# Scores in row halves with a 0/1 mask product, and a fixed order of engines and PSUM banks, in an attention and mixer kernel

## The chip, the cores and the metric

The kernel runs on one core of a Trainium2 chip. The metric is the device time of the slowest (here the only) core in microseconds, as the median of several executions. The span that a profile shows is some 2 us shorter than that execution's time, because it runs from the first to the last instruction of the program.

## The reference, cut to what matters

Two stages follow one another. The first is attention over 4 batches of 8 heads with 768 positions and head dimension 64, under a mask made of 32-position blocks. The second is a mixer on each batch: a product of rank 32 along the sequence, then a two-layer perceptron of widths 512, 2048 and 512.

```python
scores = scale * np.matmul(q, k.transpose(0, 1, 3, 2))      # 768 x 768 for each of 32 heads
scores = np.where(mask, scores, -1000000000.0)              # mask: 24 x 24 blocks of 32 x 32
attn = np.exp(scores - scores.max(-1, keepdims=True)); attn /= attn.sum(-1, keepdims=True)
x = np.matmul(attn, v)                                      # then heads side by side: 768 x 512
u = x + (x^T U V)^T                                         # rank 32
out = u + relu(u @ w_ch1) @ w_ch2
```

The kernel handles two heads at a time, a "pair": 16 pairs, four to a batch. While the pairs of batch b go through attention, the perceptron of batch b-1 runs in between.

## The kernel before

The mask lies in the contraction. A head's queries and keys have 64 rows. Below or above them stand 24 rows: a one-hot code of the block on one side and -240 for each block that is masked on the other. One matmul over all 128 rows then gives score plus mask, and one exponential of ScalarE finishes it (scale 0.125).

```python
drows = [slice(0, D), slice(D, P)]            # rows of head 0 and of head 1: D = 64, P = 128
mrows = [slice(D, D + NB), slice(0, NB)]      # the 24 mask rows of each
def scores(i, h, g):                          # 128 keys of one head, all 768 queries
    psc = pscp.tile([P, 2, 512], FP32, tag="psc", name="psc")       # two PSUM banks, two buffers
    for c in range(2):
        nc.tensor.matmul(psc[:, c, 0:HS],                           # HS = 384
            kT[:, h, g * P : (g + 1) * P], qT[:, h, c * HS : (c + 1) * HS], start=True, stop=True)
    nc.scalar.activation(out=est[:, g]..., in_=psc[:, :, 0:HS], func=AF.Exp, scale=0.125)
```

The other large parts are the value products (128x65), the two layers of the perceptron (`w1` with 384 columns, `w2` with 512), the relus, dealt by turns to ScalarE and VectorE, and the small steps of the mixer. Program order on TensorE is fixed by slots: one score step, then whatever is due. PSUM comes from three pools, and the order on the other engines is the scheduler's.

```python
def w1(jj, c):                                # ... four matmuls into one bank, then
    if c == 0: nc.scalar.activation(out=dst, in_=pt, func=AF.Relu)
    else:      nc.vector.tensor_scalar_max(out=dst, in0=pt, scalar1=0.0)
for h in range(2):                            # ... in the loop over pairs
    for g in range(T):
        pair.ests[h] = scores(i, h, g)
        at(slot - g + AVSLOT[g], lambda ...: pair.av(h, g))         # value products some slots later
        run_due()                             # ... and perceptron steps of the batch before
```

The softmax here doesn't subtract the row's maximum and nothing guards it: scores larger than these inputs give would overflow.

Of the kernel before, what the change touches and what calls it, by code (L numbers as in the profile page):

```python
# [16 lines left out]
P = 128  # L17
# [3 lines left out]
def kernel(  # L21
# [29 lines left out]
    NST = 2  # L51
# [14 lines left out]
    oh_np = np.zeros((P, T, D), dtype=np.float16)  # L66
    oh_np[cols % P, cols // P, blk] = 1.0

# [11 lines left out]
    oh_dr = nc.inline_tensor(oh_np, name="onehot_const")  # L80
# [6 lines left out]
    epool = ctx.enter_context(tc.tile_pool(name="epool", bufs=2))  # L87
    xpool = ctx.enter_context(tc.tile_pool(name="xpool", bufs=2))
    upool = ctx.enter_context(tc.tile_pool(name="upool", bufs=2))
    tpool = ctx.enter_context(tc.tile_pool(name="tpool", bufs=18))  # L90
# [3 lines left out]
    pscp = ctx.enter_context(  # L94
        tc.tile_pool(name="pscp", bufs=2, space=bass.MemoryType.PSUM)
    )
    psvp = ctx.enter_context(
        tc.tile_pool(name="psvp", bufs=1, space=bass.MemoryType.PSUM)
    )
    psmp = ctx.enter_context(  # L100
        tc.tile_pool(name="psmp", bufs=3, space=bass.MemoryType.PSUM)
    )

    def psm(shape, dtype):
        return psmp.tile(shape, dtype, tag="pm", name="pm")

    id16 = consts.tile([P, P], FP16)
    oh = consts.tile([P, T, D], FP16)
# [6 lines left out]
    qst = [consts.tile([P, 2, T, P], FP16, name=f"qst{i}") for i in range(NST)]  # L115


# [4 lines left out]
    kst = [consts.tile([P, 2, T, P], FP16, name=f"kst{i}") for i in range(NST)]  # L122
# [6 lines left out]

    def load_qk(i):  # L130
        b, hp = divmod(i, HP)
        last = None
        for src, st, nm in ((q, qst, "qld"), (k, kst, "kld")):
            ld = ldpool.tile([P, 2, T, D], FP32, tag="ld" + nm, name=nm)
            nc.sync.dma_start(
                out=ld,
                in_=src[b, 2 * hp : 2 * hp + 2].rearrange("h (p t) d -> p h t d", t=T),
            )
            if i < NPE:
                sts[i, nm] = stpool.tile([P, T, 2, D], FP16, tag="st" + nm, name="st" + nm)  # L140
                dst = sts[i, nm].rearrange("p t h d -> p h t d")
            else:
                dst = st[i % NST][:, :, :, 0:D]
            last = nc.gpsimd.tensor_copy(out=dst, in_=ld)  # L144
        return last

    def load_v(i):
        b, hp = divmod(i, HP)
        ld = ldpool.tile([P, 2, T, D], FP32, tag="ldv", name="vld")
        nc.sync.dma_start(  # L150
            out=ld,
            in_=v[b, 2 * hp : 2 * hp + 2].rearrange("h (p t) d -> p h t d", t=T),
        )
        nc.gpsimd.tensor_copy(out=vts[b % 2][:, 2 * hp : 2 * hp + 2, :, 0:D], in_=ld)  # L154
# [27 lines left out]
    for tile_ in (Ut, Vt):  # L182
        nc.gpsimd.memset(tile_, 0.0)
# [7 lines left out]
    def first_turn(h, n, c):  # L191
# [3 lines left out]
        elif c == 0:  # L195
            pt = pw[:, 1, 0:HS]
        else:
            pt = pscp.tile([P, 2, 512], FP32, tag="psc", name="psc")[:, 0, 0:HS]
# [9 lines left out]
    with tc.manual_schedule(  # L208
# [5 lines left out]
        pw = pscp.tile([P, 2, 512], FP32, tag="psc", name="psc")  # L214
# [7 lines left out]
        pks = [psvp.tile([P, HS], FP32, tag="pv", name="pv"), psm([P, HS], FP32)]  # L222
# [77 lines left out]

    def mask_columns():
        def both(ap):
            return ap[:, None].broadcast_to([P, 2, T, D])

        nc.sync.dma_start(out=oh, in_=oh_dr.ap())
        pb = psm([P, T, D], FP32)
        for t in range(T):
            nc.tensor.matmul(
                pb[:, t, :], ohT[:, t * P : (t + 1) * P], bias[0:NB, 0],
                start=True, stop=True,  # L310
            )
        nc.vector.tensor_copy(out=kst[0][:, 0, :, D:], in_=pb)
        nc.gpsimd.tensor_copy(out=kst[0][:, 1, :, D:], in_=kst[0][:, 0, :, D:])
        for i in range(NST):
            nc.gpsimd.tensor_copy(out=qst[i][:, :, :, D:], in_=both(oh))
            if i > 0:
                nc.gpsimd.tensor_copy(out=kst[i][:, :, :, D:], in_=kst[0][:, :, :, D:])
# [29 lines left out]

    def front(i):
        augs[i] = (qres[i % 2], kres[i % 2])
        for st, aug in zip((qst, kst), augs[i]):  # L350
            last = nc.sync.dma_start_transpose(
                aug.rearrange("d h (t p) -> d (h t) p", t=T),
                st[i % NST].rearrange("p h t d -> p (h t d)"),
# [23 lines left out]
    ests = {}  # L377

    def scores(i, h, g):
        qT, kT = augs[i]  # L380
        if g == 0:
            ests[h] = epool.tile([P, T, S], FP16, tag="est", name="est")
        est = ests[h]
        psc = pscp.tile([P, 2, 512], FP32, tag="psc", name="psc")
        for c in range(2):
            nc.tensor.matmul(  # L386
                psc[:, c, 0:HS],
# [5 lines left out]
            out=est[:, g].rearrange("k (c n) -> k c n", c=2), in_=psc[:, :, 0:HS],  # L393
            func=AF.Exp, scale=0.125,
        )
        return est

    class Batch:
        def __init__(self):
            self.xf = xpool.tile([P, T, HD], FP32, tag="xf", name="xf", bufs=3)  # L400
# [5 lines left out]
            self.tT = []  # L406


    class Pair:
        def __init__(self, i, bt):  # L410
            self.b, self.hp = divmod(i, HP)
            self.bt = bt
            self.ests = {}
            self.pu = {}
            self.xh = xpool.tile([P, T, P], FP16, tag="xh", name="xh", bufs=3)
            self.ch = slice(self.hp * P, (self.hp + 1) * P)
            self.xbar = NPE <= i < NPAIR - 1

        def av(self, h, g):

            head = 2 * self.hp + h
            if g == 0:
                self.pav = psvp.tile([P, T, D + 1], FP32, tag="pv", name="pv")
            pav, est = self.pav, self.ests[h]
            for sc in range(T):
                nc.tensor.matmul(  # L426
                    pav[:, sc, :],
                    est[:, g, sc * P : (sc + 1) * P],
                    vts[self.b % 2][:, head, g, 0 : D + 1],
                    start=(g == 0 and sc == 0), stop=(g == T - 1),  # L430
                    skip_group_check=True,
                )
            if g == T - 1:
                rcp = misc.tile([P, T], FP32, tag="rcp", name="rcp")
                nc.vector.reciprocal(out=rcp, in_=pav[:, :, D])  # L435
                for dst in (
                    self.xh[:, :, h * D : (h + 1) * D],
                    self.bt.xf[:, :, head * D : (head + 1) * D],
                ):
                    self.last = nc.vector.tensor_tensor(  # L440
                        out=dst, in0=pav[:, :, 0:D],
                        in1=rcp[:, :, None].broadcast_to([P, T, D]), op=ALU.mult,
                    )

        def mix(self):
            pa = psm([P, P], FP32)
# [5 lines left out]
            nc.vector.tensor_copy(out=self.bt.a16[:, self.ch], in_=pa)  # L452


        def ut_x(self, c):
            pu = self.pu[c] = psm([P, HS], FP32)
            for j in range(3):
                nc.tensor.matmul(
                    pu[:, j * P : (j + 1) * P], self.xh[:, 3 * c + j, :], id16,
# [3 lines left out]
        def ut_a(self, c):  # L463
# [6 lines left out]
            nc.vector.tensor_copy(  # L470
                out=self.bt.uT[self.hp][:, c * HS : (c + 1) * HS], in_=self.pu[c]
            )


        def add(self, c):
            if c == 0:
                self.u16 = xpool.tile([P, T, P], FP16, tag="u16", name="u16")
            pu = psm([P, 3, P], FP32)
# [7 lines left out]
            nc.vector.tensor_add(out=self.u16[:, ts, :], in0=self.xh[:, ts, :], in1=pu)  # L486
            nc.vector.tensor_add(out=xf, in0=xf, in1=pu)  # L487
            if c == 1 and self.xbar:
                nc.sync.dma_start_transpose(
                    self.bt.uT[self.hp].rearrange("c (t p) -> c t p", t=T),  # L490
                    self.u16.rearrange("p t c -> p (t c)"),
                )

        def turn(self):
            pt = psm([P, S], FP16)
# [4 lines left out]
            nc.vector.tensor_copy(out=self.bt.uT[self.hp], in_=pt)  # L500


    def mlp_steps(b, bt):
        def w1(jj, c):
            if c == 0:
                bt.tT.append(tpool.tile([P, S], FP16, tag="tT", name="tT"))
            pt = psm([P, HS], FP32)
            for cc in range(NCC):
                nc.tensor.matmul(  # L509
                    pt,  # L510
                    w1t[:, cc, jj * P : (jj + 1) * P],
                    bt.uT[cc][:, c * HS : (c + 1) * HS],
                    start=(cc == 0), stop=(cc == NCC - 1),
                )
            dst = bt.tT[jj][:, c * HS : (c + 1) * HS]
            if c == 0:
# [4 lines left out]
        hold = {}  # L521

        def w2(sc, part):
            if part == 0:
                hold[sc] = psm([P, HD], FP32)
                if b == 0:
                    nc.tensor.matmul(  # L527
                        hold[sc], Vt[:, sc, :], bt.a16, start=True, stop=False
                    )
            for jj in range(4 * part, 4 * part + 4):  # L530
                nc.tensor.matmul(  # L531
                    hold[sc],
                    bt.tT[jj][:, sc * P : (sc + 1) * P],
                    w2t[:, jj, :],
                    start=(b > 0 and jj == 0), stop=(jj == NJJ - 1),
# [193 lines left out]
```

## Time and profile before

| | before |
|---|---|
| time, median | 298.92 us (298.86 to 299.38) |
| PE busy, as the page models it | 98% |
| sum of all matmul spacings if none waited | 283 us |
| lost between the first and the last matmul start | 9.3 us, of which 7.7 us before 50 us |
| VectorE (DVE), ScalarE (ACT) busy | 142.0 us, 179.8 us |

The first fence is from the page of the kernel before: the span, the busy times of the engines, and the shares of the chain that ended last.

```profile
span 296.7 us, 6622 instructions
PE 291.4 (98%) x2775; PEld 182.3 (61%) x2775; DVE 142.0 (48%) x299; ACT 179.8 (61%) x261; POOL 50.2 (17%) x70
PE 87%; ACT 12%; issue 0%; DVE 0%
```

TensorE's work ends the kernel in 87% of the chain. But a busy PE is modelled, since matmuls overlap. The next lines are the costliest groups of the page (line, engine, operation, tiles, shapes, count; then busy us, mean ns of one, and idle time before them).

```profile
L392 ACT ACTIVATE est<-psc 128x768 f16<-128x768 f32 x192 | 149.6, 812 | 51.6 <-PE psc L386 50.7
L509 PE MATMUL pm<-uT,w1t 128*128 128x384 f16 x512 | 94.6, 326 | 0.0
L386 PE MATMUL psc<-qres,kres 128*128 128x384 f16 x384 | 93.5, 325 | 1.0 <-ACT est L392 0.7
L531 PE MATMUL pm<-w2t,tT 128*128 128x512 f16 x368 | 90.7, 379 | 0.0
L426 PE MATMUL pv<-vt,est 128*128 128x65 f16 x1152 | 55.7, 193 | 0.0
```

The mean of one matmul (325 ns for 384 columns) is its time from start to end, not what it costs in a stream. The cost is the distance to the next start. In the trace that is 162 ns for 384 columns, 215 ns for 512, 55 ns for 128 and 29 ns for 65. All "sums" below use these distances, and a "wait" is what a start comes later than that. The 384 score matmuls are thus 62 us.

The table by stretches shows where the kernel is bound by what. Its columns are the busy time of each engine, the clock, the DMA share and the rate.

```profile
core 0: us, PE busy (x) PEld busy (x) DVE busy (x) ACT busy (x) POOL busy (x), PEclk, DMA share, GB/s
0.00:16.00 16.00, 14.49 (x143) 8.52 (x144) 11.78 (x25) 12.34 (x18) 8.98 (x17) 1.00 0.75 239
16.00:44.00 28.00, 27.70 (x403) 20.99 (x401) 19.78 (x45) 27.98 (x40) 14.09 (x20) 1.00 0.90 255
50.00:297.00 247.00, 243.18 (x2165) 148.65 (x2162) 106.04 (x220) 134.41 (x197) 23.69 (x29) 1.00 0.46 114
```

From 16 to 44 us ScalarE is busy 27.98 of 28 us: the first batch has no perceptron to hide behind, so its exponentials set the pace. After 50 us only PE is full.

Two stretches of PE's timeline will be needed later (start us, length us, group, count, and in brackets a wait with its releaser). Six products with 24-row operands (they put mask values in columns) cost a gap before and after, although nothing holds them.

```profile
32.04 0.48 PE L386 MATMUL psc<-qres,kres 128*128 128x384 f16 x2
32.46 0.34 PE L308 MATMUL pm<-bias,small 24*128 24x64 f16 x6
32.74 0.35 PE L426 MATMUL pv<-vt,est 128*128 128x65 f16 x6
...
6.61 0.48 PE L386 MATMUL psc<-qres,kres 128*128 128x384 f16 x2
6.93 0.50 PE L281 MATMUL pm<-id,stqld 128*128 128x128 f16 x6
7.26 0.49 PE L386 MATMUL psc<-qres,kres 128*128 128x384 f16 x2
```

Two 384-column matmuls from 32.04 us are done streaming at 32.36 us, yet the 24-row ones start at 32.46. The six of them need 0.17 us, yet the next start is at 32.74. In the single records the gaps are 93 and 92 ns.

### The profile page before, as it was taken

The page shows a single profiled execution, that of the slowest core. Times are in us where ns is not written, and L with a number is a line of the kernel's source. Part 1 is how long each engine was busy: PE and PEld are TensorE (multiplying, and loading weights), DVE is VectorE, ACT ScalarE, POOL GpSimd, SP SyncE. Part 2 cuts the span into 40 slices and gives each one's busy share as a digit, 9 for nine tenths or more (in the row PEclk, how much of TensorE's full clock was granted, in tenths as well). Part 3 has the DMA queues.
Part 4 walks back from the last instruction along what each step waited for, and adds up shares of the span by engine and source line. Part 5 has one row for each costly group of instructions (what it writes and reads, how often), then busy time and mean ns, then how long its engine had stood idle before and what let it go on. Part 6 is the DMA issues. An engine that isn't in the chain of part 4 may idle for free.

```text
span 296.7 us, 6622 instructions
## 1 busy us (share of the span) xinstructions
PE 291.4 (98%) x2775; PEld 182.3 (61%) x2775; DVE 142.0 (48%) x299; ACT 179.8 (61%) x261; POOL 50.2 (17%) x70
## 2 busy tenths in 40 slices
PE   8999999999999999999999999999999999999995
PEld 3677776666666555666665556666665655565444
DVE  7766776346452525454452624346462535443112
ACT  5999997587766655767775555777875530332000
POOL 4773184014031212030201203030000000000000
PEclk9999999999999999999999999999999999999999
DMA  6899949096959494744719385662510121000111
GB/s 192 288 315 235 295 154 144 8 254 94 170 187 231 136 225 139 163 139 72 224 29 240 121 178 198 141 188 43 92 29 35 39 62 73 36 0 2 71 71 71
DMA packets 58661, 39.94 MB, mean 135 GB/s; under 512 B 40152, under 2 KB 55144, under 8 KB 58632
## 3 DMA queue, kind: packets, MB, share of 16 engines
q1 hardware_dynamic: 55764, 35.19, 43.9%
q0 software_dynamic: 2688, 4.19, 8.3%
q8 instruction: 21, 0.34, 0.5%
q10 hardware_dynamic: 180, 0.15, 0.1%
q14 instruction: 8, 0.07, 0.1%
HBM read 27.72 MB, written 6.29 MB: 115 GB/s over the span
## 4 chain that ended last, share of the span: by engine, by line
PE 87%; ACT 12%; issue 0%; DVE 0%
PE pm L509 28%; PE pm L531 27%; PE psc L386 16%; ACT est L392 12%; PE pv L426 9%; PE pm L448 1%; PE psc L218 1%; PE pm L481 1%; PE pm L550 1%; PE pm L527 0%; PE pm L497 0%; PE pm L364 0%; PE pm L201 0%; PE psc L201 0%; DVE of L555 0%
## 5 line engine op out<-in xcount | busy, mean ns | idle before, releaser
L392 ACT ACTIVATE est<-psc 128x768 f16<-128x768 f32 x192 | 149.6, 812 | 51.6 <-PE psc L386 50.7
L509 PE MATMUL pm<-uT,w1t 128*128 128x384 f16 x512 | 94.6, 326 | 0.0
L386 PE MATMUL psc<-qres,kres 128*128 128x384 f16 x384 | 93.5, 325 | 1.0 <-ACT est L392 0.7
L531 PE MATMUL pm<-w2t,tT 128*128 128x512 f16 x368 | 90.7, 379 | 0.0
L509 PEld LDWEIGHTS <-w1t 128*128 128x128 f16 x512 | 47.1, 98 | 27.0 <-issue 0.2
L426 PEld LDWEIGHTS <-est 128*128 128x128 f16 x1152 | 51.9, 97 | 16.5
L519 DVE TENSOR_SCALAR tT<-pm 128x384 f16<-128x384 f32 x64 | 35.6, 556 | 51.3 <-PE pm L509 48.6
L426 PE MATMUL pv<-vt,est 128*128 128x65 f16 x1152 | 55.7, 193 | 0.0
L517 ACT ACTIVATE tT<-pm 128x384 f16<-128x384 f32 x64 | 31.4, 490 | 38.2 <-PE pm L509 25.5
L386 PEld LDWEIGHTS <-kres 128*128 128x128 f16 x384 | 36.0, 97 | 27.0 <-issue 1.9
L531 PEld LDWEIGHTS <-tT 128*128 128x128 f16 x368 | 33.3, 98 | 30.1
L144 POOL CAST qst<-qld 128x768 f16<-128x768 f32 x10 | 8.3, 827 | 120.5 <-DMA qld<-in_q_dram 120.5
L539 DVE TENSOR_TENSOR of<-xf,pm 128x512 f32<-128x512 f32 x23 | 15.7, 684 | 25.9 <-PE pm L531 25.9
L435 DVE RECIPROCAL rcp<-pv 128x6 f32<-128x6 f32 x32 | 6.1, 192 | 38.1 <-PE pv L426 38.1
L440 DVE TENSOR_TENSOR xh<-pv,rcp 128x384 f16<-128x384 f32 x32 | 17.8, 557 | 1.0
L486 DVE TENSOR_TENSOR u<-xh,pm 128x384 f16<-128x384 f16 x24 | 13.2, 551 | 9.8 <-PE pm L481 9.3
L440 DVE TENSOR_TENSOR xf<-pv,rcp 128x384 f32<-128x384 f32 x32 | 17.5, 547 | 0.0
L154 POOL CAST vt<-vld 128x768 f16<-128x768 f32 x16 | 13.3, 828 | 14.7 <-DMA vld<-in_v_dram 14.2
L487 DVE TENSOR_TENSOR xf<-xf,pm 128x384 f32<-128x384 f32 x24 | 13.1, 547 | 0.0
L452 DVE CAST a<-pm 128x128 f16<-128x128 f32 x16 | 4.7, 291 | 15.9 <-PE pm L448 15.8
L144 POOL CAST kst<-kld 128x768 f16<-128x768 f32 x10 | 8.3, 827 | 5.1 <-DMA kld<-in_k_dram 5.1
L448 PE MATMUL pm<-xh,Ut 128*128 128x128 f16 x96 | 8.0, 219 | 0.0
(75 smaller groups left out, 111.2 us busy)
## 6 DMA issues: line engine op xcount, KB each, us to landing
vld<-in_v_dram SPq DMA_DIRECT2D x16, 384.0 KB, 5.3
out_dram<-of SPq DMA_DIRECT2D x23, 256.0 KB, 2.0
qld<-in_q_dram SPq DMA_DIRECT2D x15, 384.0 KB, 4.6
kld<-in_k_dram SPq DMA_DIRECT2D x15, 384.0 KB, 5.0
w1t<-in_moe_w_ch_dram POOLq DMA_DIRECT2D x4, 512.0 KB, 10.6
w2t<-in_moe_w_ch_dram POOLq DMA_DIRECT2D x4, 512.0 KB, 6.3
qld<-in_q_dram SPq DMA_DIRECT2D x2, 192.0 KB, 3.3
kld<-in_k_dram SPq DMA_DIRECT2D x2, 192.0 KB, 3.3
```

Source lines behind the costliest of these rows:

```text
L144: last = nc.gpsimd.tensor_copy(out=dst, in_=ld)
L154: nc.gpsimd.tensor_copy(out=vts[b % 2][:, 2 * hp : 2 * hp + 2, :, 0:D], in_=ld)
L386: nc.tensor.matmul(psc[:, c, 0:HS], kT[:, h, g * P : (g + 1) * P], qT[:, h, c * HS : (c + 1) * HS], start=True, stop=True,)
L392: nc.scalar.activation(out=est[:, g].rearrange("k (c n) -> k c n", c=2), in_=psc[:, :, 0:HS], func=AF.Exp, scale=0.125,)
L426: nc.tensor.matmul(pav[:, sc, :], est[:, g, sc * P : (sc + 1) * P], vts[self.b % 2][:, head, g, 0 : D + 1], start=(g == 0 and sc == 0), st ...
L440: self.last = nc.vector.tensor_tensor(out=dst, in0=pav[:, :, 0:D], in1=rcp[:, :, None].broadcast_to([P, T, D]), op=ALU.mult,)
L486: nc.vector.tensor_add(out=self.u16[:, ts, :], in0=self.xh[:, ts, :], in1=pu)
L509: nc.tensor.matmul(pt, w1t[:, cc, jj * P : (jj + 1) * P], bt.uT[cc][:, c * HS : (c + 1) * HS], start=(cc == 0), stop=(cc == NCC - 1),)
L517: nc.scalar.activation(out=dst, in_=pt, func=AF.Relu)
L519: nc.vector.tensor_scalar_max(out=dst, in0=pt, scalar1=0.0)
L531: nc.tensor.matmul(hold[sc], bt.tT[jj][:, sc * P : (sc + 1) * P], w2t[:, jj, :], start=(b > 0 and jj == 0), stop=(jj == NJJ - 1),)
L539: nc.vector.tensor_add(out=of, in0=bt.xf[:, sc, :], in1=hold[sc])
```

## The change

The intent: from the second batch on (pairs 4 to 15) the mask leaves the contraction. A head's scores then need 64 rows only, so that two heads fit into the array at once, one in each half of its rows. The mask becomes a 0/1 tile in SBUF, and VectorE multiplies the exponentials with it. With PE so relieved, the order on PE, VectorE, ScalarE and the DMA queue is written out in full as a plan that a search has found, and so is the PSUM bank of every product. The loads of a later pair are issued behind the crossbar transpose of the pair before. GpSimd's casts of the later pairs are also cut into pieces of 192 columns. The core of the diff:

```diff
+    PS = psum.tile([P, 8, 512], FP32, name="ps")          # all eight banks, placed by hand
+    def psm(shape, dtype):
+        ring["psm"] += 1
+        return bank((7, 2, 5)[ring["psm"] % 3], shape, dtype)
+    def half_quad(i, j, hs):                              # 256 keys of the heads hs
+        units[h] = PS[:, 3 * h : 3 * h + 3, :]...         # head 0: banks 0 to 2, head 1: 3 to 5
+        for u, lo, hi in ((0, 0, 512), (0, 512, S), (1, 0, 256), (1, 256, S)):
+            for h in hs:
+                nc.tensor.matmul(units[h][:, u * S + lo : u * S + hi],
+                    kT[drows[h], g * P : (g + 1) * P], qT[drows[h], lo:hi], ...)
+        for h in hs:
+            "e": nc.scalar.activation(out=both[h], in_=units[h]..., func=AF.Exp, scale=0.125)
+            "p": nc.vector.tensor_mul(out=both[h], in0=both[h], in1=mask[:, 2 * j : 2 * j + 2, :])
+    def mask_part(g, c, n):                               # 12 of these, in the first batch
+        nc.tensor.matmul(pm, kmask[:, g * P : (g + 1) * P], qres[0][:, 0, c * HS : (c + 1) * HS], ...)
+        "k": nc.vector.tensor_single_scalar(out=mask[...], in_=pm, scalar=-1.0, op=ALU.is_ge)
+    PLAN = """
+    S R7 e S t A A e S v R2 e S t A7 A e S M5 e S m X2 A e S Y A e S y A X6 e S Y K2 e S y k A
+    ... (22 lines in all)
+    W e e d W p W6 f p Q U7 e e W b W p U7 p Q a W e e U7 f p U0 a V6 b p Q v V7 e e U6 v p U0 a
+    """
-    def mask_columns(): ...                               # mask columns for the crossbar, gone
-            if c == 0: nc.scalar.activation(out=dst, in_=pt, func=AF.Relu)
-            else: nc.vector.tensor_scalar_max(out=dst, in0=pt, scalar1=0.0)
+            if engine == "a": ...Relu on ScalarE...  else: ...on VectorE...
```

In the plan a capital letter is a product on PE and its digit the PSUM bank. Q is a score step of both heads, H of one head, U and W are the two layers of the perceptron, V and A value products, R transposes of queries or keys, K a mask product, M, X, Y, D the mixer. A small letter is the work on its result: e an exponential, p a mask multiply, a and b a relu on ScalarE or VectorE. There are 34 Q and 4 H, 86 a and 42 b.

## The prediction

> **What bounds the kernel now.** TensorE. The page gives PE 98% busy, and PE busy is modelled, so I read spacings: 384-column matmuls start every 162 ns, 512-column ones every 215 ns, the 65-column value products every 29 ns. Summed over all 2775 matmuls that is 283 us; the last one ends at 293.2 us. Only 9.3 us are lost: 4.8 us in the first 20 us, 3.0 us between 20 and 60 us, and about 0.15 us in each later 20 us. In the chain of waits the first batch (7 to 41 us) follows ScalarE's exponentials (every 0.70 us); afterwards it is PE nearly throughout. DVE (48%) and ACT (61%) have room.
>
> **What the change removes, adds, moves.**
> 1. Scores of pairs 4 to 15 contract over 64 rows instead of 128 (the mask rows go), and the two heads lie in the two row halves of the array. 34 of 36 steps issue both heads together, into different PSUM banks. The Trainium skill ("TensorEngine Tiling (Array Packing)", Key Properties) says tiles run in parallel, but changing the tiling mode drains the engine. No pair of row halves is in this trace, but the drain is: entering and leaving the six 24-row mask matmuls at 32 us cost 92 ns each. Eight 384-column-equivalent matmuls, 1.30 us, become about 0.65 us plus 0.18 us of drains: 0.47 us saved, 34 times = 15.8 us. The two steps with single heads (four calls) lose 0.7 us.
> 2. Twelve mask products add 1.9 us of PE, partly in slack of the ScalarE-bound first batch; mask columns (0.35 us) and 18 PE transposes less two (about 0.7 us) go.
> 3. Exponentials of 12 pairs double in width: by the slope between 384 (490 ns) and 768 columns (812 ns), about 1.46 us for 1536. ACT gets 86 of 128 relus instead of 64 and still totals about 190 us.
> 4. DVE gains 72 fp16 mask multiplies of 1536. The skill ("VectorE: DVE Perf Modes", the perf-mode tier table) gives two elements a cycle for 16-bit tensor_tensor in SBUF; the trace has only the 16-bit PSUM copies (768 in 557 ns) at that rate. Estimate 0.9 us each, 65 us; DVE total about 198 us, about 83% of PE's work between the first and last paired step: the tight place.
> 5. Order and banks: PE hardly waited after 50 us before, so this protects the gain rather than adding one.
>
> **On the critical path.** PE's items: about 14 us net, plus perhaps 1 us of early waits. A PE sum without new waits gives about 279 us. I add 4 us: short score-to-score cycles (PE 3.6 to 3.9 us, while two exponentials plus latency need as much), batch boundaries, and imperfect overlap of the halves.
>
> **Predicted: 283 us, range 278 to 293.** Faster by over 2%: 0.86; within 2%: 0.10; slower: 0.04.
>
> **What would show it.** Matmul starts of the two heads nearly together, 64-row scores costing 0.8 us per step including drains; gaps near 90 ns before and after each; ACT groups of 128x1536 near 1.45 us; DVE multiplies near 0.9 us; DVE near 70% of the span; PE waits after 50 us totalling under 6 us.
>
> **What would make it wrong.** Halves that do not overlap: the span then stays near 300 us. Multiplies at one element per cycle (1.75 us), or slowed by GpSimd casts: DVE would bind, over 300 us. One late DVE result or crossbar landing stalling PE's fixed order repeatedly.

## The result, and the profile after

The changed kernel takes 289.46 us (288.51 to 289.75, 4 runs), the kernel before 298.89 us: ratio 0.967, 95% interval 0.9645 to 0.9695. A ratio is the mean time of one kernel's runs over that of the other's of the same rounds, so it is not quite the ratio of the medians quoted. The gain is 9.4 us where 15.9 us were predicted. The time lies in the range on record, 6.5 us above the 283 us named.

These are the page's lines of the changed kernel that answer to those of before.

```profile
span 286.7 us, 6705 instructions
PE 278.7 (97%) x2769; PEld 164.2 (57%) x2769; DVE 196.2 (68%) x354; ACT 178.5 (62%) x211; POOL 66.6 (23%) x157
PE 83%; DVE 5%; DMA 5%; ACT 3%; SPq 3%; POOL 1%; issue 1%; DVEq 0%; ACTq 0%
```

PE still ends the kernel, and VectorE has grown by 54 us. The groups of the new work, with different shapes kept apart:

```profile
L713 ACT ACTIVATE est<-ps 128x1536 f16<-128x1536 f32 x72 | 100.7, 1449 | 38.5 <-PE ps L704 28.6 <-DVE of L611 8.3 <-DVE xh L481 1.3
L719 DVE TENSOR_TENSOR est<-est,mask 128x1536 f16<-128x1536 f16 x72 | 68.7, 957 | 15.4 <-ACT est L713 15.3
L704 PE MATMUL ps<-qpl,kpl 64*128 64x512 f16 x144 | 29.2, 381 | 0.0
L704 PE MATMUL ps<-qpl,kpl 64*128 64x256 f16 x144 | 14.5, 269 | 0.0
```

The exponential of double width costs 1449 ns and the multiply 957 ns, close to the estimates. The table by stretches, same columns and bounds as before:

```profile
0.00:16.00 16.00, 12.75 (x118) 7.30 (x119) 10.78 (x23) 10.74 (x16) 9.26 (x18) 1.00 0.73 232
16.00:44.00 28.00, 27.65 (x402) 20.79 (x399) 23.14 (x52) 27.57 (x38) 13.08 (x21) 1.00 0.90 257
50.00:287.00 237.00, 232.48 (x2206) 132.91 (x2204) 157.02 (x272) 135.48 (x154) 38.61 (x108) 1.00 0.39 104
```

In the first 16 us PE and ScalarE did less than before (118 matmuls against 143, 16 ScalarE instructions against 18): something at the start went wrong there. PE's timeline shows one paired step, then the start of the first pair.

```profile
78.69 0.81 PE L603 MATMUL ps<-w2t,tT 128*128 128x512 f16 x3
79.43 0.82 PE L704 MATMUL ps<-qpl,kpl 64*128 64x512 f16 x8
80.19 0.82 PE L576 MATMUL ps<-uT,w1t 128*128 128x384 f16 x4
...
6.59 0.48 PE L397 MATMUL ps<-qres,kres 128*128 128x384 f16 x2
8.70 0.49 PE L294 MATMUL ps<-id,stqld 128*128 128x128 f16 x6 [1.63 <-DVE kres L246]
9.03 0.81 PE L397 MATMUL ps<-qres,kres 128*128 128x384 f16 x4
```

The step's eight matmuls (3072 columns) take 0.76 us from their first start to the next work. In the single records they start in twos: 3 to 4 ns apart, then 223, 106, 106 ns later, and after the last of 512 columns 308 ns pass to the next start, 92 more than it needs. The gap ahead of the step is 96 ns. The start is the other finding: the transposes that before started at 6.93 us now stand until 8.70 us, held by VectorE.

Summed over the trace, in us from the first matmul's start to the last one's:

| | before | after |
|---|---|---|
| 128-row score matmuls | 62.2 | 15.6 |
| 64-row score steps, with the gap behind them | - | 29.4 |
| gap ahead of them | - | 3.7 |
| all other matmuls | 220.6 | 221.7 |
| waits, before 16 us / 16 to 50 us / after 50 us | 4.3 / 3.4 / 1.7 | 5.8 / 2.8 / 3.4 |
| sum | 292.1 | 282.3 |

The work fell by 12.5 us and the waits grew by 2.7 us.

### The profile page after: what moved, and what is told of

Same layout as the page of the kernel before. It is cut to its first block, busy times and chain, and to the rows that moved or that the text cites. A ratio compares the mean times of both kernels' runs of the same rounds, so it can differ in the third digit from the quotient of the medians.

```text
span 286.7 us, 6705 instructions
## 1 busy us (share of the span) xinstructions
PE 278.7 (97%) x2769; PEld 164.2 (57%) x2769; DVE 196.2 (68%) x354; ACT 178.5 (62%) x211; POOL 66.6 (23%) x157
## 4 chain that ended last, share of the span: by engine, by line
PE 83%; DVE 5%; DMA 5%; ACT 3%; SPq 3%; POOL 1%; issue 1%; DVEq 0%; ACTq 0%
PE ps L576 27%; PE ps L603 24%; PE ps L413 11%; PE ps L704 8%; PE ps L679 4%; DMA out_dram<-of 2%; PE ps L507 2%; ACT est L403 2%; DMA kld<-in_k_dram 2%; SPq L350 2%; PE ps L541 1%; PE ps L623 1%; PE ps L654 1%; DVE xh L481 1%; DVE kres L246 1%; PE ps L640 1%
## 5 line engine op out<-in xcount | busy, mean ns | idle before, releaser
L713 ACT ACTIVATE est<-ps 128x1536 f16<-128x1536 f32 x72 | 100.7, 1449 | 38.5 <-PE ps L704 28.6
L576 PE MATMUL ps<-uT,w1t 128*128 128x384 f16 x512 | 94.3, 326 | 0.1
L603 PE MATMUL ps<-w2t,tT 128*128 128x512 f16 x368 | 88.7, 379 | 0.0
L719 DVE TENSOR_TENSOR est<-est,mask 128x1536 f16<-128x1536 f16 x72 | 68.7, 957 | 15.4 <-ACT est L713 15.3
L586 ACT ACTIVATE tT<-ps 128x384 f16<-128x384 f32 x86 | 41.7, 493 | 47.3 <-PE ps L576 45.6
L413 PE MATMUL ps<-vt,est 128*128 128x65 f16 x1152 | 43.0, 193 | 0.5 <-DVE of L611 0.5
L588 DVE TENSOR_SCALAR tT<-ps 128x384 f16<-128x384 f32 x42 | 23.2, 555 | 27.5 <-PE ps L576 26.7
L704 PE MATMUL ps<-qpl,kpl 64*128 64x512 f16 (+1 forms) x288 | 31.3, 325 | 0.0
L688 ACT ACTIVATE est<-ps 128x768 f16<-128x768 f32 x36 | 26.3, 810 | 0.4 <-PE ps L679 0.4
L481 DVE TENSOR_TENSOR xh<-ps,rcp 128x384 f16<-128x384 f32 x32 | 17.8, 557 | 1.1
L144 POOL CAST vt<-vld 128x192 f16<-128x192 f32 x40 | 15.1, 420 | 3.8 <-DMA vld<-in_v_dram 2.3
```

The source lines that it names most:

```text
L144: last = nc.gpsimd.tensor_copy(out=dst[:, h, ts], in_=ld[:, h, ts])
L413: nc.tensor.matmul(pav[:, sc, :], est[:, n, sc * P : (sc + 1) * P], vts[b % 2][:, 2 * hp + h, g, 0 : D + 1], start=(g == 0 and sc == 0), s ...
L481: self.last = nc.vector.tensor_tensor(out=dst, in0=pav[:, :, 0:D], in1=rcp[:, :, None].broadcast_to([P, T, D]), op=ALU.mult,)
L576: nc.tensor.matmul(pt, w1t[:, cc, jj * P : (jj + 1) * P], bts[b].uT[cc][:, c * HS : (c + 1) * HS], start=(cc == 0), stop=(cc == NCC - 1),)
L603: nc.tensor.matmul(po, tts[b, c, jj][:, s * P : (s + 1) * P], w2t[:, jj, :], start=(b > 0 and jj == 0), stop=(jj == NJJ - 1), skip_group_c ...
L688: lambda: nc.scalar.activation(out=dst, in_=ps[:, :, 0:HS], func=AF.Exp, scale=0.125),
```

## The experiments

My theory after this reading: the gain is the two halves running at once; the gaps around a step are the price of changing the array's mode; the order and the banks do not win time but keep waits away; and of what was missed, part lies in the first 20 us. Rivals: the gain is the searched order; what was missed is VectorE, now near full.

### Pairing: e2_unpaired, then e5_same_half

```diff
 # e2_unpaired
-        half_quad(i, j, (0, 1))
+        half_quad(i, j, (0,))
+        half_quad(i, j, (1,))
```

> The changed kernel, but in the 34 paired steps all four matmuls of head 0 are issued before the four of head 1; everything else, order, banks, engines, 64 rows, stays. My theory: the gain is the two row halves running at once. Only the last piece of head 0 can then overlap the first of head 1, so a step grows from 0.757 us to about 1.19 us: 34 times 0.43 is 14.6 us, giving 300 to 305 us, slower than before. Rival: the gain is the searched order and the smaller number of rows as such; then the time stays below 293 us.

Measured: 288.93 us (288.48 to 290.22), ratio 0.9662. Taken at its word, that would have decided for the rival. The trace says that the edit did not do what it was meant to do:

```profile
79.51 0.83 PE L704 MATMUL ps<-qpl,kpl 64*128 64x512 f16 x8
80.28 0.82 PE L576 MATMUL ps<-uT,w1t 128*128 128x384 f16 x4
```

The step still takes 0.77 us. The program has 512, 256, 256, 512 columns of head 0 and then the same of head 1. In the single records the starts are 13 ns apart, then 214, then 13, 96, 13, 96, 13 ns, with widths 512, 512, 256, 256, 256, 256, 512, 512: head 1's first matmul starts 13 ns after head 0's first, ahead of three that stand before it in the program. (A build of this kernel shows that the compiled program keeps that order, so no scheduler has mixed the heads.) In the trace each half takes its own next product. So the order of issue in a step made no difference here, and the experiment is no test of the pairing. The next one puts both heads in the same half.

```diff
 # e5_same_half (head 1 gets head 0's scores: wrong on purpose)
-                    kT[drows[h], g * P : (g + 1) * P],
-                    qT[drows[h], lo:hi],
+                    kT[drows[0], g * P : (g + 1) * P],
+                    qT[drows[0], lo:hi],
```

> The run e2_unpaired did not undo the pairing: its trace shows the two heads' matmuls still starting 13 ns apart, against program order. Here both heads of every step read rows 0 to 63 (head 1 gets head 0's scores, so the result is wrong on purpose); order, banks, sizes and drains are those of the changed kernel, but both heads now need the same half of the array. My theory, the halves at once are the gain: a paired step takes about 1.30 us plus the drain in place of 0.757 us, 34 times 0.64 is 22 us at most and 18 us if drains and waits absorb some: 305 to 311 us, slower than before. Rival, the gain is the searched order and the missing waits: below 296 us.

Measured: 309.99 us (309.16 to 310.38), ratio 1.0351, slower than before the change. The groups of the score matmuls, same shapes and counts as in the changed kernel:

```profile
L704 PE MATMUL ps<-qpl,kpl 64*128 64x512 f16 x144 | 43.7, 379 | 0.0
L704 PE MATMUL ps<-qpl,kpl 64*128 64x256 f16 x144 | 21.8, 269 | 0.0
```

One matmul lasts as long as before (379 against 381 ns), but the time covered by all of them grows from 29.2 and 14.5 us to 43.7 and 21.8 us. A paired step takes 1.403 us against 0.757 us; 34 times 0.646 us is 22.0 us, and 20.5 us of it appear in the time (1.3 us of other waits vanish in the slack). This settles the pairing: without two halves at once the change loses, and with the gap of 92 ns taken off both, the halves run 1.97 times as fast. A warning by the way: this kernel passed the comparison with the reference although the scores of head 1 are wrong in 12 of 16 pairs. The inputs make the scores so small (within about 0.06 of zero before the mask) that the weights are nearly even. The comparison does see the mask: e3_nomul below, which drops it, fails by 0.71.

### The gaps: e6_drains

```diff
+            if (u, lo) == (1, 0):       # between the two key blocks of a step; overwritten later in it
+                nc.tensor.matmul(units[hs[-1]][:, 2 * S - 64 :], kT[:, 0:P], qT[:, 0:64],
+                    start=True, stop=True, skip_group_check=True)
```

> The changed kernel with one 128-row matmul of 64 columns put between the two score blocks of each of the 38 steps, into columns that the step overwrites afterwards (result unchanged). It adds two changes of the tiling mode a step. My theory, a change costs about 0.095 us each way wherever it stands: 38 times about 0.21 us, 8 us: 296 to 298 us. Rival, the 96 and 92 ns gaps are the wait for the previous matmul's end and weight load that would be there anyway or hide behind other waits: less than 3 us.

Measured: 297.69 us (296.88 to 298.23), ratio 0.9942. PE's timeline of one step:

```profile
83.03 0.50 PE L709 MATMUL ps<-qpl,kpl 64*128 64x512 f16 x4
83.46 0.20 PE L704 MATMUL ps<-qpl,kpl 128*128 128x64 f16 x1
83.59 0.50 PE L709 MATMUL ps<-qpl,kpl 64*128 64x256 f16 x4
84.02 0.82 PE L576 MATMUL ps<-uT,w1t 128*128 128x384 f16 x4
```

The step takes 0.99 us (83.03 to 84.02) in place of 0.76 us: 0.23 us for a matmul that needs 0.03 us. 38 times 0.23 us is 8.7 us; 8.2 us came. No run put a 64-row product in the same place, but inside a step products follow each other without such a gap. The changed kernel's 38 steps therefore pay about 38 times 0.19 us, 7.2 us, for changing between 128-row and 64-row work. That is a third of what the halves could win.

### VectorE: e3_nomul, e4_alternate, e8_alt_nomul

```diff
 # e3_nomul (wrong on purpose)
-                then("p", lambda: nc.vector.tensor_mul(out=both[h], in0=both[h], in1=mask[...]))
+                then("p", lambda: None)
 # e4_alternate: relus by turns, 64 and 64; e8_alt_nomul: both edits
-                results["relu"].popleft()(kind)
+                ring["relu"] = ring.get("relu", 0) + 1
+                results["relu"].popleft()("ba"[ring["relu"] % 2])
```

> The changed kernel without the 72 mask multiplies (the result is wrong on purpose). My theory: VectorE is near full but mostly in time; PE waits put down to VectorE after 50 us come to about 1.7 us, so 1 to 2 us are won at most: 287.5 to 288.5 us. Rival: VectorE is the new bound and holds back what the prediction missed: then 4 us or more are won, 285 us or less.

Measured: 288.54 us (288.2 to 289.86), ratio 0.965. Taking 69 us of work off VectorE wins less than 1 us, which is not told apart from nothing. VectorE is not what holds the changed kernel.

> The changed kernel with the relus dealt to ScalarE and VectorE by turns, 64 each, as before the change, in place of the searched 86 and 42. VectorE gets 22 more of 0.556 us (12.2 us), ScalarE 22 fewer of 0.49 us. My theory: PE is the bound and the engine order only protects it: 1 to 4 us longer, 290.5 to 293.5 us. Rival: the engine assignment is unimportant: within 0.5 us of 289.5. Second rival, VectorE bound: 8 us longer or more.

Measured: 301.36 us (300.45 to 302.6), ratio 1.0081. My theory's number was wrong by far: 12 us are lost, though VectorE gets only 12.2 us more work (22 relus of 0.556 us) in 290 us, and ScalarE is relieved. PE's waits:

```profile
PE ps L704 <- DVE tT L588: 3.7, 5, 2.1
PE ps L576 <- ACT tT L586: 3.7, 4, 1.5
PE ps L576 <- DVE tT L588: 2.1, 2, 1.7
```

All three are relus that come late, on either engine. Is it their load or their place?

> The relus dealt by turns as in e4_alternate, and no mask multiplies as in e3_nomul (result wrong on purpose). e4_alternate was 12 us slower, e3_nomul alone won nothing. If the 12 us are VectorE's fixed queue running late under its load, taking 69 us of multiplies off it brings the time back to 288 to 291 us. If they come from ScalarE and VectorE in the wrong places of the order, whatever the load, it stays above 296 us.

Measured: 295.42 us (294.92 to 295.85), ratio 0.9868, between the two stories. Without multiplies the waits for VectorE's relus shrink to 1.1 and 0.4 us, but those for ScalarE's stay at 3.7 us to the digit. So about 6 of the 12 us are VectorE's queue running late under its load. The other 6 us are not one thing: 3.7 us are relus that now stand behind two exponentials of 1.45 us on ScalarE, where the plan had them on VectorE (all four in the trace), 1.5 us are relus of VectorE that come late even without the multiplies, and 1.3 us are a wait for a GpSimd cast near 20 us, which the changed kernel's profile does not have. In this plan each engine works its list in order, and a bank is free only when its relu has come up. That e3 wins nothing and e4 loses 12 us belong together: the plan is fitted tightly to this deal, and both engines are on time but not early.

### The banks: e10_banks

From the first paired step on, every product takes bank 6 or 7 by turns, another only where both are in use; 167 of 252 places change, the order of the work does not.

```diff
-    Y A y A y A A A Q v e e M6 X7 m Y R6 y p H t U7 e p H a U6 e p U0 b U7 b U6 p b Q a R6 e e
-    U7 t U6 b p U0 a V7 b p Q v V6 e e U7 v p H a U6 e p M5 b U7 m U3 a p U2 a X7 D6 a H d Y D0
+    ... U6 p b Q a R7 e e
+    U6 t U7 b p U6 a V7 b p Q v V6 e e U7 v p H a U6 e p M7 b U6 m U7 a p U6 a X7 D2 a H d Y D6
```

> The changed kernel with the searched PSUM banks undone from the first paired step on: every product takes bank 6 or 7 by turns, and another bank only where both are in use; order and engines stay. 167 of 252 placements move. My theory: the searched banks win nothing themselves but keep PE from waiting for evictions (a relu eviction with its latency takes longer than the 0.65 us of the product in between), above all where many products of the first layer follow each other: 3 to 10 us longer than the changed kernel, 292 to 300 us. Rival: the banks do not matter, within 1 us of 289.

Measured: 323.67 us (323.35 to 324.05), ratio 1.0806: 34 us more than the changed kernel. The direction is as expected, the size is three times the most that I allowed. Waits after 50 us go from 3.4 to 37 us; the largest of PE's:

```profile
PE ps L575 <- DVE xf L480: 6.5, 12, 1.2
PE ps L575 <- ACT est L712: 3.7, 5, 1.1
PE ps L575 <- DVE of L610: 2.5, 2, 1.8
```

First-layer products wait for the bank of a value product until VectorE has divided it (L480), and for relus behind exponentials. The paired steps themselves gain just as much as in the changed kernel. A gain on PE of 12.5 us would have been lost nearly three times over by this choice of banks. It is a harsh one: the plan spreads the 219 placed products of this part over all eight banks, the run puts 183 of them into two and uses four in all. A ring of three banks, like the pool of the kernel before, was not tried, and no run undoes the order of the work by itself.

### The loads: e11_loads

```diff
-                    loads(self.i + 1)          # behind the crossbar transpose of pair i
-        if i <= HP:
-            loads(i)
+        loads(i)                               # at the pair's first score step
```

> The changed kernel with the loads (and the crossbar transposes of queries and keys) of pairs 5 to 15 issued at the pair's first score step, not behind the crossbar transpose of the pair before. They come a little earlier or up to a few us later, and three score steps still lie between them and their use. My theory: DMA has slack after 50 us and this part is worth nothing by itself: within 0.7 us of 289. Rival: it orders the crossbar ahead of the loads, so that without it the first-layer products wait for transposed rows: 2 us longer or more.

Measured: 289.04 us (287.95 to 290.62), ratio 0.9655 (0.9617 to 0.9693), not told apart from the changed kernel. This part of the change is worth nothing that shows. DMA's share after 50 us is 0.39.

### The start: e1_ring, e7_start

```diff
 # e1_ring
-        return bank((7, 2, 5)[ring["psm"] % 3], shape, dtype)
+        return bank((2, 5, 7, 5, 7, 2, 5)[ring["psm"] - 1], shape, dtype)
```

> The changed kernel, but the seven evictions of the start take the three rotating PSUM banks in another order, so that the transposes of the second head go into a bank that ScalarE has already emptied. My theory: in the changed kernel they wait 1.79 us (6.75 to 8.70 us) for VectorE to empty the mask rows from the same bank; ScalarE's second exponential is then 1.75 us late, and the first batch, which follows ScalarE, hands this delay on whole. Expected: PE wait gone, second exponential near 7.8 us, time about 1.7 us shorter than the changed kernel: ratio to before about 0.962, near 287.7 us. Rival: the first batch has slack elsewhere (mask products, loads), and the time stays at 289.5 us within 0.4.

Measured: 288.9 us (288.04 to 289.85), ratio 0.9655. The wait was gone, and the second exponential came 0.71 us after the first instead of 2.45 us (at 8.31 us, against 9.56 us in the changed kernel). But the time hardly moved, because PE met the next wait:

```profile
15.49 0.48 PE L679 MATMUL ps<-qres,kres 128*128 128x384 f16 x2
18.21 0.51 PE L654 MATMUL ps<-id,stqld 128*128 128x128 f16 x6 [2.23 <-POOL stqld L141]
```

The plan turns pair 2's queries right behind pair 1's first score. Their load lands about then, behind the copy of mask rows that the change put ahead of it in the queue. In the changed kernel's trace this cast began at 15.60 us, in e1_ring's at 17.32 us, although its load was issued within 0.1 us of the same time; why the load took longer is not shown. It does not come every time: two of the four executions took 288.0 and 288.2 us, two 289.6 and 289.9 us, and the profiled one is of the slower two. So the second wait has to go as well:

```diff
 # e7_start: the ring of e1_ring, and
-    S R7 e S t A A e S v R2 e S t A7 A e S M5 e S m X2 A e S Y A e S y A X6 e S Y K2 e S y k A
+    S e S A A e S v R5 e S t A7 A e S M5 R2 e S m t X6 A e S Y A e S y A X2 e S Y K6 e S y k A
-        nc.sync.dma_start(out=kmask[mrows[0], :], in_=kres[0][mrows[0], 0, :])   # ahead of the loads
+        ... the same behind loads(0)
```

> The run e1_ring took the bank wait away (PE reached its first value products 1.2 us earlier), but PE then stood 2.39 us for the cast of pair 2's queries, whose transposes the plan puts right behind pair 1's first score and whose load the mask-row copy delays. Here: the ring order of e1_ring, pair 2's two transposes moved two and one scores later into other banks, and the mask-row copy issued behind the loads. My theory, both waits gone: PE waits before 22 us fall from 5.7 us to about 3.5 us, and the time is 1.5 to 2.5 us shorter than the changed kernel, 287 to 288 us. Rival, the loads at the start bound the first batch and any earlier start is lost to them: within 0.5 us of 289.

Measured: 287.64 us (287.34 to 288.01), ratio 0.9606, interval 0.9589 to 0.9623, clear of the changed kernel's 0.9645 to 0.9695. PE's timeline at the two places:

```profile
6.94 0.50 PE L294 MATMUL ps<-id,stqld 128*128 128x128 f16 x6
...
17.48 0.51 PE L653 MATMUL ps<-id,stqld 128*128 128x128 f16 x6 [0.55 <-POOL stqld L141]
```

The transposes start at 6.94 us as before the change, and the cast is 0.55 us late in place of 2.23 us. The cast itself began at 16.59 us, still later than in the changed kernel (15.60 us), so it is not shown that moving the mask-row copy helps; the transposes were also moved later. By the medians 1.8 us are won, as expected. Between the two profiled executions it is only 0.6 us (288.51 and 287.92 us): the changed kernel's profile fell on its fastest execution, e7_start's on a slow one. In these two, PE's waits before 16 us fell by 1.3 us, and those between 16 and 50 us rose by 0.4 us.

### A version meant to beat both: e9_best, e12_start_store

e9_best adds three things to e7_start: pair 2's transposes later still, a third buffer for output rows, and two single-head steps joined to a paired one.

```diff
-    tc.tile_pool(name="opool", bufs=2)
+    tc.tile_pool(name="opool", bufs=3)
-    S e S A A e S v R5 e S t A7 A e S M5 R2 e S m t X6 A e S Y A e S y A X2 e S Y K6 e S y k A
+    S e S A A e S v e S A7 A R5 e S M6 m t e S R2 X6 e S t A A Y e S y A X5 e S Y K6 e S y k A
-    ... R6 y p H t U7 e p H a U6 e p U0 b U7 b U6 p b Q a R6 e e
+    ... R6 y p t U7 p a U6 Q e e b U7 b p U0 b p U6 Q a R6 e e
```

> A version meant to beat both kernels, built on e7_start: the transposes of pair 2 one score later still, with the small steps around them dealt to other banks (the cast was still 0.71 us late, and VectorE 0.36 us); the first two single-head steps joined to one paired step (two steps of 0.85 us with their drains become one of 0.85 us); and three instead of two buffers for the finished output rows, for the VectorE wait on a store that stands behind crossbar transposes and loads (PE lost 0.4 to 1.3 us to it at 182 us in every run so far). If PE's sum of work and waits is the bound, each term counts: 1.0, 0.85 and 0.7 us less than e7_start, 285 to 286.5 us. If the joined step stalls on its six banks or the start is bound by the loads, 287 to 288 us as e7_start.

Measured: 288.7 us (288.59 to 288.99), ratio 0.9641, worse than e7_start. The joined step saved its 0.85 us of PE but brought waits of 0.48, 0.69 and 1.00 us between 45.8 and 50.9 us: in the trace first-layer products wait there, twice for copies of VectorE and once for the joined step's two exponentials. The two single-head steps had filled part of that time. The wait at 182 us, 0.92 us in e7_start, was gone. The last run keeps only that buffer.

> e7_start with three instead of two buffers for the finished output rows, nothing else: of e9_best's three additions this is the one whose wait vanished in its trace (the 0.92 us before value products at 182 us, put down to VectorE waiting for a store), while the joined step cost 2.2 us of new waits near 46 to 51 us for 0.85 us saved, and the moved small steps cost 1.1 us of waits on VectorE at 21.5 and 27.5 us. If the store wait was a real cost on PE's path, 0.5 to 1.0 us less than e7_start: ratio to before about 0.958, near 286.8 us. If it was hidden or comes back elsewhere, 287.6 us, ratio 0.9606.

Measured: 287.35 us (287.18 to 289.01, 5 runs), ratio 0.9623 (0.96 to 0.9647). Four of five executions lie at or below e7_start's median, one at 289.01, so the two are not told apart. In its trace the wait at 182 us is gone and the last matmul starts 0.72 us earlier. The fastest version shown is e7_start or this one, about 0.6% under the changed kernel.

## Why the prediction was right or wrong

- **PE is the bound, and the halves run at once: right.** Shown by e5_same_half (20.5 us lost without it). A step cost 0.757 us plus 0.096 us ahead of it, 0.853 us, against 0.83 us predicted.
- **The drains: right, and read from the trace of before.** 92 ns at the six 24-row products before, 96 and 92 ns around each step after; e6_drains doubles them and pays. The Trainium skill ("TensorEngine Tiling (Array Packing)", Key Properties) says that a change of mode drains the engine. The trace gives the size and agrees: even the weight load of a step's first product begins only at the end of the gap (79.43 us in the step shown), while inside a stream it begins one product ahead.
- **The sum of PE's work: about right.** 14.2 us less predicted, 12.5 us measured. Score work with its gaps fell by 13.6 us where 15.1 us were predicted: a paired step saves 0.44 us and not 0.47 us (0.9 us in 34), and 0.6 us are waits inside three steps.
- **The multiply at two elements a cycle: right.** VectorE's fp32 additions of 256 and 512 columns (421 and 685 ns) show 1.03 ns an element and 157 ns fixed. At half of that an element, 1536 elements would take 949 ns; measured are 957 ns. This is the rate in the Trainium skill, "VectorE: DVE Perf Modes", the perf-mode tier table. VectorE's total is 196 us against 198 us; ScalarE's is 178.5 us, where about 190 us were predicted.
- **VectorE as the tight place: wrong as a bound, right as a warning.** e3_nomul wins nothing; e4_alternate shows that there is no room for a worse deal.
- **"A PE sum without new waits gives about 279 us": this is the step that failed.** My own terms did not give it: 298.9 less 14 less 1 is 283.9. The record does not hold the working of the 279 us; it comes out if only the 5 us of waits of the first 20 us are kept, the 0.8 us before the first matmul left out, and the other 4 us of old waits taken to vanish. They did not: the first batch still follows ScalarE. Waits came to 12.0 us between the first and last matmul start, where this working has about 9 with the 4 us added for new ones. With the sum put right, the same terms give 288 us. Of the 6.5 us missed, 3 are these waits, 1.7 are work, 0.8 the omitted start, and 1 is that the profiled execution (288.51 us) was the fastest of four.
- **Waits after 50 us "under 6 us": right,** 3.4 us. **"Perhaps 1 us of early waits" won: wrong.** A fixed bank ring made the second head's transposes wait 1.8 us at 7 us (e1_ring). That this costs time is shown only together with the wait for pair 2's queries (e7_start).
- **"This protects the gain rather than adding one" of the order and banks: right for the banks** by e10_banks, which also shows how much there was to protect against a choice of few banks: 34 us. For the engine of each relu, e4_alternate shows 12 us. The order of the products was not undone by any run.

Open: a mean granted clock of 0.987 to 0.994 shows in two of the changed kernel's four executions, and in 16 of 36 over all kernels that keep its start; in e7_start, e9_best and e12_start_store, which do not, it is at least 0.998 in all 13. Whether PE's long wait at the start lowers the clock for a while was not tried by itself (e10_banks keeps that start and shows 0.999 or more in four; e1_ring, with the bank wait gone, shows 0.994 in one of four).

## What to carry to other kernels

When a contraction fills only half of the array's rows, two independent products in the two halves cost one, but each change of mode costs some 0.19 us both ways, so put as many half-row products as PSUM holds between two changes. When PE is relieved, what had slack becomes just on time, and another choice of banks (34 us here) or of engines (12 us) can lose more than the new idea wins (9.4 us). In a prediction, add up old waits and work separately and let the waits stay unless you can name what removes each.

## What the Trainium skill lacked or had wrong

- "TensorEngine Tiling (Array Packing)", Key Properties, says that changing the tiling mode drains the engine and gives no figure. Here it costs 96 ns into and 92 ns out of 64-row work, and 93 and 92 ns for the 24-row products at 32 us; an extra pair of changes in each of 38 steps cost 8.2 us, with the small product that made them.
- The same page, Theoretical Speedup, says up to 2 times for half the rows. The runs show 1.97 times inside a step (1.31 against 0.665 us without the closing gap), and 1.52 times (1.296 against 0.853 us) for a step of eight matmuls with its gaps.
- "TensorE: Matmul & The Clock Gate", Part 3, says that matmuls start and end strictly in program order. In e2_unpaired head 1's first matmul started 13 ns after head 0's first, ahead of three matmuls of head 0 that precede it in the program, in all 34 steps. (Δstart of 3 to 4 ns for neighbours of different halves agrees with the page's 4 ns.)
- "SBUF — State Buffer", Who interferes with whom, says that a VectorE instruction with two SBUF inputs contends with GpSimd reads, and that the shared port pair is an exclusive lock. One direction agrees: in the changed kernel a 192-column GpSimd cast takes some 348 ns clear of the mask multiplies, but 1066 to 1112 ns when it starts 36 to 227 ns into one, and then ends 200 to 207 ns after it. The other direction does so only in part: of ten multiplies that started within a cast, the two that came 64 and 76 ns after its start took 1093 and 1076 ns, and the eight that came 194 to 256 ns after it took 941 to 959 ns, as did the multiplies that met no cast (947 to 959 ns). The profile's GpSimd times are rough.
